# Sliding-window attention with a soft mixture of experts: score groups of 64 queries and eight heads instead of 128 queries and four heads

## The chip, the cores and the metric

The kernel runs on one core of a Trainium2 chip. The metric is device time in microseconds (us) of one execution; lower is better. The engines are called as in the profile: PE is the matrix engine, PEld its loading of the stationary operand (the weights of a matmul), DVE the vector engine, ACT the scalar engine, POOL the GpSimd engine, SP the engine that issues most DMAs.

## What is computed

Batch 8, 8 heads, 576 positions, head size 64. Attention looks back over a window of 128 keys with a bias that grows with the distance, one slope a head; its output, 4608 tokens of 512 values, goes through a soft mixture of 8 experts with 4 slots each.

```python
def _attn_ref(q, k, v):
    B, H, S, D = q.shape
    window = 128
    scale = 1.0 / np.sqrt(D)
    scores = scale * np.matmul(q, k.transpose(0, 1, 3, 2))
    pos = np.arange(S)
    rel = pos[:, None] - pos[None, :]
    slopes = 2.0 ** (-8.0 * (np.arange(H, dtype=np.float32) + 1) / H)
    bias = slopes[:, None, None] * (-np.abs(rel).astype(np.float32))[None, :, :]
    mask = (rel >= 0) & (rel < window)
    scores = np.where(mask, scores + bias[None], -1000000000.0)
    scores = scores - np.max(scores, axis=-1, keepdims=True)
    attn = np.exp(scores)
    attn = attn / (np.sum(attn, axis=-1, keepdims=True) + 1e-09)
    return np.matmul(attn, v).astype(np.float32)

def _moe_ref(x, phi, w1, w2):            # x: tokens, 4608 x 512
    logits = x @ phi                     # 32 slots: 8 experts of 4
    d = softmax of logits over the tokens
    slot_input = d.T @ x
    per expert e: slot_out[e] = relu(slot_input[e] @ w1[e]) @ w2[e]
    c = softmax of logits over the slots
    return c @ slot_out
```

(The last function is written out in short.)

## The kernel before

**Two parts.** The front (up to about 212 us) is attention, with the routing of the experts woven in; the tail loads the last expert weights, runs the experts and combines. Instructions of PE, DVE, ACT, POOL and SP run in the order in which the code emits them (`manual_schedule`), each engine waiting in order for what it needs.

**Groups.** `groups` lists the units of attention: batch b, tile t of 128 positions (t = 4 is the tail of 64), and g. For t < 4, g picks two of the four head pairs, so a group is 128 queries by four heads; t = 4 has one group of 64 queries by eight heads. There are 72 groups: 16 with t = 0, 48 with t = 1 to 3, 8 with t = 4. A head pair sits on the partitions: the even head's 64 dimensions on 0 to 63, the odd one's on 64 to 127 (`half`).

**Scores** (`scores`, L237 to L269) go to a PSUM tile `s4` of four slots (u = 2 x parity + pair) of 256 columns, two banks, double-buffered. For t > 0 the queries are cut into four strips of 32; strip c occupies partitions 32c to 32c+31 and gets the scores of its 160 keys (five blocks of 32) at columns 32c to 32c+159. So the row of query p uses key columns of the previous tile beyond p, and of its own tile up to p. First 8 matmuls of `ramp` with `ones` write the bias (L259), then 16 matmuls of 64 x 32 weights add the scores (L266). An fp32 matmul is two instructions in the profile, each with its weight load. For t = 0 there is no previous tile: 2 bias matmuls (L247) and 4 score matmuls of 64 x 128 weights (L252).

**Softmax.** `merge` on DVE makes one 128-column row of the 256 by a copy under a mask: 128 columns a slot for t = 1 to 3 (L281), 64 for t = 4 (L283); for t = 0 it overwrites the keys above the diagonal with a constant `low` (L279). Then DVE takes the row maximum (L301), scales it (L304), ACT computes the exponentials with their row sums, one slot at a time (`expo`, L357), POOL adds an epsilon (L309), DVE inverts (L313) and multiplies (`normalise`, L317).

**Values.** `flip` turns the four slots on PE (L372), ACT copies them to `pa` (L379), POOL separates the previous tile's part (`pp`, L381) from the own part (`pa`, L383; L386 and L388 for t = 4). `values` (L410) multiplies: for each key tile, pair and parity one matmul, weights 128 keys by 64 dimensions of V, moving 128 queries (64 for t = 4). `x_store` copies a finished tile of x (L426), `x_flip` turns it (L438), `x_keep` copies (L447), and `logits`, `token_*`, `slot_*` do the routing once in four tiles.

**Order.** In iteration i of the main loop DVE gets merge(i), row maximum(i), inverse(i-1), bias(i), normalise(i-1); ACT gets split(i-3) (i-2 in the first iterations), stores and copies of x, then expo(i); PE gets flip(i-3), values(i-4), scores(i+1), then what routing has fallen due. Scores(i+1) needs the PSUM buffer of group i-1, and so its exponentials. The last groups are written out by hand behind the loop; there the weights' loads go into areas that attention has given up (`place`), in an order of their own.

Of the kernel before, what the change touches and what calls it, by code (L numbers as in the profile page):

```python
# [23 lines left out]
NS = E * SPE  # L24
# [11 lines left out]
WIN = P + KB  # L36
NB = S // KB
HW = 512
CW = P + TAIL + NS
WARM = 6  # L40
# [28 lines left out]
def tile_attn_softmoe(  # L69
# [20 lines left out]
    mask_u = cst[:, 0:P].bitcast(I32)  # L90
    mask_t = cst[:, P:P + TAIL].bitcast(I32)
# [14 lines left out]
    ramp = cpool.tile([P, 2, 2, WIN], BF16, name="ramp")  # L106
# [4 lines left out]
    qs = [kq[:, NB * P + 2 * P * i:NB * P + 2 * P * i + 2 * P] for i in range(3)]  # L111
# [61 lines left out]
    def load_q(i, eng=None):  # L173
        b, t, g = groups[i]
        o = 4 * P * t + 2 * P * g
        (eng or nc.sync).dma_start(qs[i % 3], qd[b, :, o:o + 2 * P])
# [29 lines left out]
    with tc.manual_schedule(engines=ORDERED):  # L206
# [6 lines left out]
        nc.gpsimd.memset(cst[:, 0:P], 1.0)  # L213
        nc.gpsimd.affine_select(cst[:, 0:P], cst[:, 0:P], [[1, P]], ALU.is_gt, 0.0, base=0, channel_multiplier=-1)
# [17 lines left out]
        nc.scalar.dma_start(cst[:, P:], cstd)  # L232
# [4 lines left out]
    def scores(i):  # L237
        b, t, g = groups[i]
        s4 = s4s[i % 2]
        parts = [s4[:, 0:2], s4[:, 2:4]]  # L240
        if i == 0:
            parts = [ps_1.tile([P, 2, 2 * P], F32, tag="xp", name="s4_0"), pq[:, 0].rearrange("p (u w) -> p u w", u=2)]
            parts = parts[::-1]
        qt = qs[i % 3].rearrange("p (j w) -> p j w", w=width(t))
        if t == 0:
            for par, rows in enumerate(half):
                nc.tensor.matmul(  # L247
                    parts[par][:, :, 0:P], lhsT=ones[rows], rhs=ramp[rows, g, :, 0:P],
                    start=True, stop=False)
            for jj in range(2):  # L250
                for par, rows in enumerate(half):
                    nc.tensor.matmul(  # L252
                        parts[par][:, jj, 0:P], lhsT=qt[rows, jj], rhs=kall[rows, 0:4, 2 * g + jj],
                        start=False, stop=(jj == 1))
        else:
            strips = [(c // 2, c % 2) if t == 4 else (g, c) for c in range(4)]
            for par, rows in enumerate(half):
                for c, (h, r) in enumerate(strips):
                    nc.tensor.matmul(  # L259
                        s4[32 * c:32 * c + 32, 2 * par:2 * par + 2, 32 * r:32 * r + WIN],  # L260
                        lhsT=ones[rows, 0:32], rhs=ramp[rows, h], start=True, stop=False)
            for jj in range(2):
                for par, rows in enumerate(half):
                    for c, (h, r) in enumerate(strips):
                        m0 = 4 * (t - 1) + r
                        nc.tensor.matmul(  # L266
                            s4[32 * c:32 * c + 32, 2 * par + jj, 32 * r:32 * r + WIN],
                            lhsT=qt[rows, 2 * h + jj if t == 4 else jj, 32 * r:32 * r + 32],
                            rhs=kall[rows, m0:m0 + 5, 2 * h + jj], start=False, stop=(jj == 1))  # L269
        st[groups[i]] = {"s4": s4, "parts": parts}  # L270

    ALL, LO, HI = slice(0, 4), slice(0, 2), slice(2, 4)

    def merge(key, us=ALL):
        t = key[1]
        s4 = st[key]["s4"]
        if t == 0:
            m = len(range(4)[us])
            nc.vector.copy_predicated(merged(key, us), bc(mask_u, 1, m), bc(low, 1, m).to_broadcast([P, m, P]))  # L279
        elif t < 4:  # L280
            nc.vector.copy_predicated(s4[:, :, P:2 * P], bc(mask_u, 1, 4), s4[:, :, 0:P])  # L281
# [841 lines left out]
```

## Time and profile before

| what | value |
|---|---|
| median of 3 runs (lowest, highest) | 289.14 us (288.57, 290.88) |
| the profiled execution | 288.49 us, span of the trace 286.0 us |
| granted TensorE clock, mean | 0.982 |
| busy share of the span: PE, PEld, DVE, ACT, POOL | 89%, 63%, 77%, 72%, 39% |
| bytes moved, mean rate | 72.61 MB, 254 GB/s |

The lines of the profile follow in the prediction. A row of instructions tells line, engine, operation, out<-in with shapes, count, then total busy us, mean ns of one, and the idle time before it with what ended that. A timeline row tells start, duration, engine, line and count, with neighbours of one kind merged. The chain of work that ended last follows the program back from its end, at each step to what released it.

### The profile page before, as it was taken

The page shows a single profiled execution, that of the slowest core. Times are in us where ns is not written, and L with a number is a line of the kernel's source. Part 1 is how long each engine was busy: PE and PEld are TensorE (multiplying, and loading weights), DVE is VectorE, ACT ScalarE, POOL GpSimd, SP SyncE. Part 2 cuts the span into 40 slices and gives each one's busy share as a digit, 9 for nine tenths or more (in the row PEclk, how much of TensorE's full clock was granted, in tenths as well). Part 3 has the DMA queues.
Part 4 walks back from the last instruction along what each step waited for, and adds up shares of the span by engine and source line. Part 5 has one row for each costly group of instructions (what it writes and reads, how often), then busy time and mean ns, then how long its engine had stood idle before and what let it go on. Part 6 is the DMA issues. An engine that isn't in the chain of part 4 may idle for free.

```text
span 286.0 us, 13588 instructions
## 1 busy us (share of the span) xinstructions
PE 253.9 (89%) x5535; PEld 178.9 (63%) x5535; DVE 221.6 (77%) x509; ACT 205.6 (72%) x817; POOL 112.9 (39%) x218
## 2 busy tenths in 40 slices
PE   8588999799979889989979998998979899999990
PEld 4366676676757567667657765766756443687750
DVE  2889989998997999988998998798973352656451
ACT  2888889988888988998898988888783411044460
POOL 2044626662573276257527725466552011000000
PEclk9689999999999999999999999999999999999997
DMA  6645368869885987969797978866574579998997
GB/s 184 218 134 164 100 197 270 276 195 289 285 271 152 305 297 233 278 224 305 218 286 242 328 236 251 278 204 219 165 265 140 169 254 365 411 393 322 362 384 282
DMA packets 36754, 72.61 MB, mean 254 GB/s; under 512 B 4402, under 2 KB 15316, under 8 KB 36692
## 3 DMA queue, kind: packets, MB, share of 16 engines
q1 hardware_dynamic: 35972, 71.24, 75.7%
q8 instruction: 43, 0.70, 1.0%
q10 hardware_dynamic: 720, 0.51, 0.6%
q14 instruction: 19, 0.16, 0.2%
HBM read 62.29 MB, written 9.44 MB: 251 GB/s over the span
## 4 chain that ended last, share of the span: by engine, by line
PE 45%; DVE 23%; ACT 16%; POOL 7%; issue 5%; DMA 2%; DVEq 0%; ACTq 0%; POOLq 0%
ACT area L357 9%; PE xp L410 7%; DVE area L317 6%; DVE s L301 6%; PE s L266 5%; PE op L967 5%; PE hp L930 5%; PE po L992 4%; DVE s L281 3%; POOL area L381 3%; PE pq L372 3%; PE lp L456 2%; DVE s L279 2%; PE s L259 2%; ACT area L379 2%
## 5 line engine op out<-in xcount | busy, mean ns | idle before, releaser
L357 ACT ACTIVATE area<-s,nb 128x128 f32<-128x128 f32 x286 | 102.7, 391 | 13.8 <-DVE nb L304 10.4
L410 PE MATMUL xp<-area 128*64 128x128 f32 (+1 forms) x1104 | 74.5, 272 | 8.4 <-POOL area L381 5.3
L357 ACT ACTIVATION_READ_ACCUMULATOR area<-s,nb 128x1 f32 x286 | 65.4, 229 | 0.0
L410 PEld LDWEIGHTS xp<-area 128*64 128x64 f32 x1104 | 54.1, 137 | 18.0 <-POOL area L381 6.1
L317 DVE TENSOR_TENSOR area<-area,rs 128x512 f32<-128x512 f32 (+1 forms) x73 | 61.0, 836 | 1.6
L301 DVE TENSOR_REDUCE s<-s 128x4 f32<-128x512 f32 x71 | 49.5, 697 | 2.2
L379 ACT COPY area<-pq 128x512 f32<-128x512 f32 (+1 forms) x72 | 43.5, 605 | 10.7 <-PE pq L372 9.0
L266 PE MATMUL s<-kq 64*32 64x160 f32 x1792 | 43.8, 302 | 2.3 <-issue 2.3
L309 POOL TENSOR_SCALAR rs<-sm 128x4 f32<-128x4 f32 x70 | 15.0, 214 | 73.0 <-ACT area L357 71.6
L383 POOL TENSOR_SCALAR_AFFINE_SELECT area<-area 128x512 f32<-128x512 f32 x48 | 41.7, 870 | 3.3
L381 POOL TENSOR_SCALAR_AFFINE_SELECT area<-area 128x512 f32<-128x512 f32 x48 | 35.5, 740 | 15.5 <-ACT area L379 14.6
L281 DVE COPY_PREDICATED s<-cst,s 128x512 f32<-128x512 int32 x48 | 33.1, 689 | 6.1 <-PE s L266 5.6
L372 PE MATMUL pq<-unit_r,area 64*128 64x64 f32 x552 | 31.3, 233 | 3.7 <-ACT area L322 2.8
L266 PEld LDWEIGHTS s<-kq 64*32 64x32 f32 x1792 | 30.1, 107 | 4.1 <-issue 3.5
L372 PEld LDWEIGHTS pq<-unit_r,area 64*128 64x128 f32 x552 | 23.3, 140 | 11.8 <-issue 3.2
L259 PE MATMUL s<-ramp,ones 64*32 64x320 bf16 x448 | 18.7, 311 | 4.8 <-ACT area L357 4.5
L426 ACT COPY area<-xp 128x512 f32<-128x512 f32 (+1 forms) x37 | 21.4, 578 | 0.2
L447 ACT COPY area<-pq 128x512 f32<-128x512 f32 x34 | 20.7, 608 | 0.3 <-PE pq L432 0.3
L438 PEld LDWEIGHTS pq<-unit_r,area 64*128 64x128 f32 x264 | 11.1, 137 | 12.8 <-issue 9.7
L994 ACT COPY ob<-po 128x512 f32<-128x512 f32 x19 | 10.4, 591 | 11.4 <-PE po L992 11.4
L994 DVE COPY ob<-po 128x512 f32<-128x512 f32 x17 | 11.2, 686 | 6.6 <-PE po L992 6.5
L438 PE MATMUL pq<-unit_r,area 64*128 64x64 f32 x264 | 15.2, 233 | 0.9 <-ACT area L379 0.6
(173 smaller groups left out, 329.1 us busy)
## 6 DMA issues: line engine op xcount, KB each, us to landing
w<-w SPq DMA_DIRECT2D x53, 512.0 KB, 5.5
out<-ob SPq DMA_DIRECT2D x36, 256.0 KB, 3.9
kq<-q_t SPq DMA_DIRECT2D x69, 128.0 KB, 3.5
kq<-k_t SPq DMA_DIRECT2D x32, 256.0 KB, 3.9
area<-v_n SPq DMA_DIRECT2D x31, 256.0 KB, 4.2
area<-w SPq DMA_DIRECT2D x8, 512.0 KB, 4.6
area<-v_n SPq DMA_DIRECT2D x12, 128.0 KB, 4.4
kq<-w SPq DMA_DIRECT2D x3, 512.0 KB, 5.9
```

Source lines behind the costliest of these rows:

```text
L259: nc.tensor.matmul(s4[32 * c:32 * c + 32, 2 * par:2 * par + 2, 32 * r:32 * r + WIN], lhsT=ones[rows, 0:32], rhs=ramp[rows, h], start=True, ...
L266: nc.tensor.matmul(s4[32 * c:32 * c + 32, 2 * par + jj, 32 * r:32 * r + WIN], lhsT=qt[rows, 2 * h + jj if t == 4 else jj, 32 * r:32 * r + 32],
L281: nc.vector.copy_predicated(s4[:, :, P:2 * P], bc(mask_u, 1, 4), s4[:, :, 0:P])
L301: nc.vector.tensor_reduce(st[key]["mx"][:, us], merged(key, us), axis=AX.X, op=ALU.max, negate=True)
L317: nc.vector.tensor_tensor(p4, p4, bc(rs, 2, P), op=ALU.mult)
L357: nc.scalar.activation(s["p4"][:, u], merged(key, u), AF.Exp, bias=s["nb"][:, u:u + 1], scale=SCALE, accum_out=s["sm"][:, u:u + 1],)
L372: nc.tensor.transpose(s["pt"][:, u, r], s["p4"][rows, u], ident[rows, rows])
L379: nc.scalar.copy(pa[:, us].rearrange("p u (r w) -> p u r w", r=2), s["pt"][:, us])
L381: nc.gpsimd.affine_select(pp[:, us], pa[:, us], [[0, m], [-1, P]], ALU.is_gt, 0.0, base=0, channel_multiplier=1)
L383: nc.gpsimd.affine_select(pa[:, us], pa[:, us], [[0, m], [1, P]], ALU.is_ge, 0.0, base=0, channel_multiplier=-1)
L410: nc.tensor.matmul(xp[D * par:D * par + D, j, 0:w], lhsT=v_slot[b, t - 1 + ph][:, D * h:D * h + D], rhs=src[:, 2 * par + i] if t < 4 else ...
L438: nc.tensor.transpose(xq[:, j, r], x[rows, j], ident[rows, rows])
```

## The change

A group of t < 4 becomes 64 queries (g picks the half of the tile) by all eight heads. The strips on the partitions are now the four head pairs; a slot (u = 2 x parity + uu) holds one block of 32 queries, uu, with its 160 keys. Slot uu starts at column 224 uu of its bank (OFF), so that the block of keys to be merged lies at the window's end for uu = 0 (block 4 onto block 0) and at its front for uu = 1 (block 7 onto block 11): 32 columns a slot for every t. For t = 0 the blocks of the missing previous tile get no scores but a large negative number, by four matmuls of a row `shut` with `ones`. Keys then lie turned by 64 in half of the slots, which `expo` sets right by reading its 128 columns as two pieces of 64 in reverse order. `flip` writes the slots sorted by uu, POOL's selection works on blocks of 32, and `values` does one matmul for each key tile and head with 64 moving columns. Bias and scores of t = 1 to 4 keep their number and shapes.

```diff
+OFF = 2 * P - KB
+QB = 2 * P
...
-        nc.gpsimd.memset(cst[:, 0:P], 1.0)
-        nc.gpsimd.affine_select(cst[:, 0:P], cst[:, 0:P], [[1, P]], ALU.is_gt, 0.0, base=0, channel_multiplier=-1)
+        nc.gpsimd.memset(shut, 0.0)
+        for par in range(2):
+            nc.gpsimd.memset(shut[64 * par:64 * par + 1, 0:P], LOW)
+        nc.gpsimd.memset(mask, 1.0)
+        for c in range(4):
+            rows = slice(KB * c, KB * c + KB)
+            nc.gpsimd.affine_select(
+                mask[rows, 0], mask[rows, 0], [[-1, KB]], ALU.is_ge, 0.0, base=0, channel_multiplier=1)
+            nc.gpsimd.affine_select(
+                mask[rows, 1], mask[rows, 1], [[1, KB]], ALU.is_gt, 0.0, base=0, channel_multiplier=-1)
...
     def scores(i):
...
+        qt = qs[i % 3].rearrange("p (j u w) -> p j u w", j=NPAIR, u=2)
+        strips = [slice(KB * c, KB * c + KB) for c in range(NPAIR)]
+        for par, rows in enumerate(half):
+            both = parts[par][:, 0:2 * OFF].rearrange("p (u w) -> p u w", u=2)
+            for c, strip in enumerate(strips):
+                nc.tensor.matmul(
+                    both[strip, :, 0:WIN], lhsT=ones[rows, 0:KB], rhs=bc(ramp[rows, c], 1, 2),
+                    start=True, stop=False)
         if t == 0:
             for par, rows in enumerate(half):
+                for uu in range(2):
+                    r = 2 * g + uu
                     nc.tensor.matmul(
+                        parts[par][:, OFF * uu:OFF * uu + WIN], lhsT=ones[rows], rhs=shut[rows, KB * r:KB * r + WIN],
+                        start=False, stop=False)
+        for uu in range(2):
+            r = 2 * g + uu
+            skip = max(4 * (1 - t) - r, 0)
+            m0 = 4 * (t - 1) + r
             for par, rows in enumerate(half):
+                for c, strip in enumerate(strips):
                     nc.tensor.matmul(
+                        parts[par][strip, OFF * uu + KB * skip:OFF * uu + WIN], lhsT=qt[rows, c, uu],
+                        rhs=kall[rows, m0 + skip:m0 + 5, c], start=False, stop=(uu == 1))
...
     def merge(key, us=ALL):
...
+        x = windows(key, us).rearrange("p a (x y) -> p a x y", y=KB)
+        m = x.shape[1]
+        nc.vector.copy_predicated(
+            x[:, :, 0:12:11, :], bc(mask.bitcast(I32), 1, m), x[:, :, 4:8:3, :])
...
     def expo(key, us=ALL):
...
+            src = merged(key, slice(2 * par, 2 * par + 2))[:, par if number[key] else 0, uu]
+            dst = s["p4"][:, u]
+            if uu != key[2]:
+                src = src.rearrange("p (a w) -> p a w", a=2)[:, ::-1]
+                dst = dst.rearrange("p (a w) -> p a w", a=2)
...
     def split(key, us=ALL):
...
+            m, i0 = own.shape[1], 2 * KB * g + KB * (us.start // 2)
             nc.gpsimd.affine_select(
+                prev, own, [[-KB, m], [0, 8], [-1, KB]], ALU.is_gt, 0.0, base=-i0, channel_multiplier=1)
             nc.gpsimd.affine_select(
+                own, own, [[KB, m], [0, 8], [1, KB]], ALU.is_ge, 0.0, base=i0, channel_multiplier=-1)
...
     def values(key, pairs=None, to=None):
...
-        inner = pairs or range(2 if t < 4 else 4)
+        inner = pairs or range(NPAIR)
         for ph in parts:
...
                     nc.tensor.matmul(
+                        xp[D * par:D * par + D, j, TAIL * g:TAIL * g + TAIL],
+                        lhsT=v_slot[b, t - 1 + ph][:, D * h:D * h + D], rhs=(pp, pd)[ph][:, :, par, j],
+                        start=(fresh and (ph, j) == (parts[0], inner[0])),
+                        stop=(done and (ph, j) == (parts[-1], inner[-1])),
                     )
...
     def x_of(b, t):
+        if (b, t) == (last, 0):
+            return halves(5)
...
-        load_weight()
         x_flip(last, 4, pq[:, 1])
         x_flip(last, 0, free[1])
+        load_weight()
         load_weight()
```

The host lays q out by half tiles to match. The tail's hand-written order keeps its steps, but for one load that now stands behind the two `x_flip`, since it fills the area that holds the last x tile now.

PE, a group of t = 0 in the second batch (rows: line, operation, out<-in, moving shape; `xp` is the output of `values`, `kq` holds q and k). Before:

```order
L247 LDWEIGHTS ones
L247 MATMUL s_1_84<-ramp,ones 128x2x128
L252 MATMUL s_1_84<-kq 128x128 x4
L372 MATMUL pq<-unit_r,area 128x64 x8
L410 MATMUL xp<-area 64x128 x8
```

And with the change (eight pairs of rows of L258, the bias, and three pairs of L265 stand ahead of these):

```order
L265 LDWEIGHTS ones
L265 MATMUL s_1_84<-cst,ones 128x160
L274 MATMUL s_1_84<-kq 32x32 x8
L274 MATMUL s_1_84<-kq 32x64 x8
L379 MATMUL pq<-unit_r,area 128x64 x8
L411 MATMUL xp<-area 64x64 x16
```

Two bias matmuls became eight, four of `shut` are new, four score matmuls became 16 narrow ones, and the eight value matmuls of the group in line behind them became 16 of half the width.

DVE, from the group (0, 4) to the first of the next batch. Before:

```order
L283 COPY_PREDICATED s_0_83<-cst,s_0_83 128x4x64
L301 TENSOR_REDUCE s_0_83<-s_0_83 128x4
L313 RECIPROCAL rs<-rs 128x4
L304 TENSOR_SCALAR nb<-s_0_83 128x4
L317 TENSOR_TENSOR area<-area,rs 128x512
L279 COPY_PREDICATED s_1_84<-cst,fine 128x4x128
```

With the change:

```order
L285 COPY_PREDICATED s_0_83<-cst,s_0_83 128x2x2x32
L301 TENSOR_REDUCE s_0_83<-s_0_83 128x2x2
L314 RECIPROCAL rs<-rs 128x4
L305 TENSOR_SCALAR nb<-s_0_83 128x4
L318 TENSOR_TENSOR area<-area,rs 128x512
L285 COPY_PREDICATED s_1_84<-cst,s_1_84 128x2x2x32
```

The order on DVE stands; both copies now move 128 elements a partition, the one of t = 0 without the constant `low` (in `fine`). The rows of t = 1 to 3 change in the same way, from 128x4x128.

More of the change, by code (lines that the diff above doesn't have):

```diff
@@ L89, in tile_attn_softmoe @@
     cst = cpool.tile([P, CW], F32, name="cst")
-    mask_u = cst[:, 0:P].bitcast(I32)
-    mask_t = cst[:, P:P + TAIL].bitcast(I32)
+    mask = cst[:, 0:2 * KB].rearrange("p (u w) -> p u w", u=2)
+    shut = cst[:, 2 * KB:2 * KB + P].bitcast(BF16)
     delta = cst[:, P + TAIL:]
@@ L110, in tile_attn_softmoe @@
     kall = kq[:, 0:NB * P].rearrange("p (n j w) -> p n j w", n=NB, j=NPAIR)
[L111 removed]
+    qs = [kq[:, NB * P + QB * i:NB * P + QB * i + QB] for i in range(3)]
     half = [slice(64 * par, 64 * par + 64) for par in range(2)]
@@ L238, in scores @@
         b, t, g = groups[i]
-        s4 = s4s[i % 2]
-        parts = [s4[:, 0:2], s4[:, 2:4]]
         if i == 0:
-            parts = [ps_1.tile([P, 2, 2 * P], F32, tag="xp", name="s4_0"), pq[:, 0].rearrange("p (u w) -> p u w", u=2)]
-            parts = parts[::-1]
-        qt = qs[i % 3].rearrange("p (j w) -> p j w", w=width(t))
+            parts = [pq[:, 0], ps_1.tile([P, 2 * QB], F32, tag="xp", name="s4_0")]
+        else:
+            parts = [s4s[i % 2][:, 2 * par:2 * par + 2].rearrange("p u w -> p (u w)") for par in range(2)]
@@ L262, in scores @@
[L262 to L269, printed above, removed]
@@ L276, in merge @@
[L276 to L281, printed above, removed]
-        else:
-            nc.vector.copy_predicated(s4[:, :, 0:TAIL], bc(mask_t, 1, 4), s4[:, :, P:P + TAIL])
-    def merged_at(key):
-        return P if 0 < key[1] < 4 else 0
-    def merged(key, us):
-        o = merged_at(key)
-        if number[key] == 0:
-            if isinstance(us, int):
-                return st[key]["parts"][us // 2][:, us % 2, 0:P]
-            return st[key]["parts"][us.start // 2][:, :, 0:P]
-        return st[key]["s4"][:, us, o:o + P]
+        x = windows(key, us).rearrange("p a (x y) -> p a x y", y=KB)
@@ L296, in rowmax, with windows @@
+        m = x.shape[1]
+        nc.vector.copy_predicated(
+            x[:, :, 0:12:11, :], bc(mask.bitcast(I32), 1, m), x[:, :, 4:8:3, :])
+    def windows(key, us):
+        if number[key] == 0:
+            return st[key]["parts"][us.start // 2].unsqueeze(1)
+        return st[key]["s4"]
+    def merged(key, us):
+        x = windows(key, us).rearrange("p a (u w) -> p a u w", u=2)
+        return x[:, :, :, 0:P]
     def rowmax(key, us):
-        if "mx" not in st[key]:
-            o = P - merged_at(key)
-            st[key]["mx"] = st[key]["s4"][:, :, o] if number[key] else work.tile([P, 4], F32, tag="mx", name="mx")
+        if "nb" not in st[key]:
```

97 lines of the change are left out of this document (36 added, 61 removed).

## The prediction

> **What bounds the kernel now.** I read the page first: the engines' shares and the chain of work that ended last.
>
> ```profile
> PE 253.9 (89%) x5535; PEld 178.9 (63%) x5535; DVE 221.6 (77%) x509; ACT 205.6 (72%) x817; POOL 112.9 (39%) x218
> ACT area L357 9%; PE xp L410 7%; DVE area L317 6%; DVE s L301 6%; PE s L266 5%; PE op L967 5%; PE hp L930 5%; PE po L992 4%; DVE s L281 3%; POOL area L381 3%; PE pq L372 3%; PE lp L456 2%; DVE s L279 2%; PE s L259 2%; ACT area L379 2%
> ```
>
> The chain passes from engine to engine; the masked copies that the change shrinks (L281, L279) hold 3% and 2% of it. The busy time by stretches comes next: the front, three pairs of t = 0 groups, and a stretch in which the chain stays on DVE.
>
> ```profile
> core 0: us, PE busy (x) PEld busy (x) DVE busy (x) ACT busy (x) POOL busy (x), PEclk, DMA share, GB/s
> 12.00:212.00 200.00, 183.52 (x4578) 134.94 (x4563) 182.54 (x402) 176.61 (x742) 105.93 (x194) 0.99 0.75 234
> 55.05:60.75 5.70, 3.94 (x98) 3.06 (x98) 5.34 (x13) 4.29 (x20) 4.37 (x7) 1.00 0.72 247
> 81.20:86.90 5.70, 3.94 (x104) 3.06 (x106) 5.35 (x12) 4.41 (x19) 4.36 (x7) 1.00 0.75 239
> 107.67:112.53 4.86, 4.53 (x122) 3.62 (x120) 4.79 (x11) 4.22 (x19) 3.09 (x6) 1.00 0.95 272
> 136.60:150.10 13.50, 12.02 (x339) 8.28 (x337) 13.28 (x32) 12.69 (x58) 5.60 (x13) 1.00 0.84 251
> ```
>
> In the front PE, DVE and ACT are busy 92%, 91% and 88%: three engines near their limit, so that relief of one is soon stopped by the next. Then the waits (us in total, times, the longest), of all engines and of PE alone:
>
> ```profile
> ACT area L357 <- DVE nb L304: 13.8, 24, 3.4
> ```
>
> ```profile
> PE xp L410 <- POOL area L381: 5.3, 6, 1.4
> PE s L259 <- ACT area L357: 4.5, 9, 1.3
> ...
> PE s L266 <- issue: 2.3, 4, 1.0
> PE xp L410 <- POOL area L383: 1.3, 4, 0.4
> ```
>
> PE waits 11.1 us (5.3 + 4.5 + 1.3) for work that comes late out of DVE by way of ACT or POOL; ACT waits 13.8 us for DVE's scaled maximum. These waits are what a faster DVE can give back.
>
> **The change, part by part. The copies.**
>
> ```profile
> L281 DVE COPY_PREDICATED s<-cst,s 128x512 f32<-128x512 int32 x48 | 33.1, 689 | 6.1 <-PE s L266 5.6
> L279 DVE COPY_PREDICATED s<-cst,fine 128x512 f32<-128x512 int32 x15 | 14.9, 997 | 0.1
> L283 DVE COPY_PREDICATED s<-cst,s 128x256 f32<-128x256 int32 x8 | 3.4, 422 | 0.3 <-PE s L266 0.3
> ```
>
> 512 elements cost 689 ns and 256 cost 422, so 267 ns per 256 and 289 ns at 128 elements, if pieces of 32 cost nothing of their own. The first group speaks for that: 256 elements in pieces of 128 took there what L283's pieces of 64 take.
>
> ```profile
> 5.86 0.43 DVE L279 COPY_PREDICATED pq<-cst,fine 128x256 f32<-128x256 int32 x1 [4.18 <-issue]
> ```
>
> The bounds are 155 ns (the line's start) and 422. L279 is dearer than L281 at the same size, and its spread is wide, 425 to 1169 ns with the half ones in it; the new copy reads PSUM under a mask, like L281, which hardly varies, so I price it by L281.
>
> ```profile
> L281 DVE COPY_PREDICATED s<-cst,s x48: 680/688/697, 10.4 to 200.6; 128x512 f32<-128x512 int32 x48
> ```
>
> ```profile
> L279 DVE COPY_PREDICATED s<-cst,fine x16: 425/1122/1169, 6.9 to 209.4; 128x512 f32<-128x512 int32 x15, 128x256 f32<-128x256 int32 x1
> ```
>
> DVE loses 48 x 0.40 = 19.2 us, 16 x 0.71 = 11.3 and 8 x 0.13 = 1.1: 31.6 us of its 182.5. On the chain L281 is 3% of 286 = 8.6 us, of which (689 - 289) / 689 = 58% go: 5.0 us. L279 is 2% = 5.7 us, of which 71% go: 4.1 us. So 9.1 us is the most that this chain gives. How much is kept depends on the neighbours. In the last stretch of the windows four copies are on the chain, the first and the last of them:
>
> ```profile
> 139.66 0.61 DVE s L281
> ...
> 146.95 0.60 DVE s L281
> ```
>
> They would save 4 x 0.4 = 1.6 us, but ACT is busy 12.69 of 13.50 us and leaves 0.8: half is kept. I take half of 5.0, 2.5 us. In the first two t = 0 pairs DVE loses 2 x 0.71 = 1.4 us; ACT needs 4.3 to 4.4 of the 5.70 us and PE, with its added work (below), 3.94 + 0.54 = 4.5: 1.2 us each is kept. In the third pair PE needs 4.53 + 0.54 = 5.07 of 4.86 us: a loss of 0.2. I take two thirds of 4.1, 2.7 us, with PE's added work on t = 0 already inside. Kept: 5.2 us.
>
> **PE, values.** t = 4 already runs the new shape, 32 instructions of 64 columns; behind a group of 16 of 128 columns:
>
> ```profile
> 60.45 1.09 PE L410 MATMUL xp<-area 128*64 128x128 f32 x16
> 61.48 0.33 PE L259 MATMUL s<-ramp,ones 64*32 64x320 bf16 x8
> 61.63 0.73 PE L266 MATMUL s<-kq 64*32 64x160 f32 x32
> ...
> 62.67 1.15 PE L410 MATMUL xp<-area 128*64 128x64 f32 x32
> 63.76 0.33 PE L259 MATMUL s<-ramp,ones 64*32 64x320 bf16 x8
> ```
>
> From start to next start, 1.03 us become 1.09: 6%. On 48 groups 2.9 us of PE, on the chain 6% of L410's 7% (20.0 us) = 1.2 us; I take 1.0. The weight loads go with it:
>
> ```profile
> 60.45 0.85 PEld L410 LDWEIGHTS xp<-area 128*64 128x64 f32 x16
> ...
> 61.51 0.53 PEld L266 LDWEIGHTS s<-kq 64*32 64x32 f32 x32
> ...
> 62.67 1.01 PEld L410 LDWEIGHTS xp<-area 128*64 128x64 f32 x32
> ```
>
> 32 loads take 1.01 us, 32 ns each, though 16 took 53 ns each: at 128 columns they waited for the matmuls. [...]
>
> **PE, scores of t = 0.**
>
> ```profile
> 105.70 0.28 PE L247 MATMUL s<-ramp,ones 64*128 64x256 bf16 x2
> ...
> 105.82 0.61 PE L252 MATMUL s<-kq 64*128 64x128 f32 x8
> ...
> 106.27 0.41 PE L438 MATMUL pq<-unit_r,area 64*128 64x64 f32 x8
> ```
>
> Now 0.57 us from start to start. After: the bias as for other tiles, 0.15 us (61.48 to 61.63); four `shut` matmuls, 640 moving columns in place of L247's 512 in 0.12 us: 0.15; 32 score instructions of 32 to 128 columns, at least the pace of their loads (0.53 us for 32), at most that of 160 columns (0.65). In all 0.83, so +0.27 us (0.25 to 0.4), 0.54 a pair, 4.3 us over 16 groups. It counts in the pairs above.
>
> **Small parts.** PE gets 1440 more matmuls (48 x 16 + 16 x 42) on 5535, each with a load. Their code comes in packets, and the four waits "issue" within the score matmuls (2.3 us) are stalls of PE with nothing else missing:
>
> ```profile
> q8 instruction: 43, 0.70, 1.0%
> ```
>
> 26% more code, 26% more such stalls: 0.6 us (0 to 2.3). [...]
>
> `values` of g = 0 now needs all columns of V. Once, at the last batch, V comes in four half loads and PE waits for it already:
>
> ```profile
> 194.39 2.64 SPq L201 DMA_DIRECT2D area<-v_n  x4
> ...
> 198.97 0.66 PE L410 MATMUL xp<-area 128*64 128x128 f32 x8 [0.90 <-DMA area<-v_n]
> ```
>
> The third and fourth issue come up to 1.3 us (half of 2.64) behind: 0 to 1.3, I take 0.5.
>
> POOL's selections go from pieces of 128 to 32; pieces of 64 cost nothing more so far:
>
> ```profile
> L381 POOL TENSOR_SCALAR_AFFINE_SELECT area<-area 128x512 f32<-128x512 f32 x48 | 35.5, 740 | 15.5 <-ACT area L379 14.6 <-PE xp L410 0.3
> L386 POOL TENSOR_SCALAR_AFFINE_SELECT area<-area 128x512 f32<-128x512 f32 x7 | 5.0, 711 | 3.9 <-ACT area L379 3.1 <-PE xp L410 0.8
> ```
>
> 0 to 10% of L381's 3% of the chain: 0 to 0.9, I take 0.2. Exponentials that read two pieces: ACT's copies of 64-column pieces and of whole rows cost the same, so 0 (up to 0.02 us x 143 = 2.9):
>
> ```profile
> L379 ACT COPY area<-pq 128x512 f32<-128x512 f32 x69 | 42.5, 615 | 9.7 <-PE pq L372 9.0
> ...
> L426 ACT COPY area<-xp 128x512 f32<-128x512 f32 x30 | 18.5, 616 | 0.1
> ```
>
> The mask's and `shut`'s making on POOL lies under the first loads; the moved load waits for two flips of PE in the tail: 0.
>
> **Sum:** -5.2 + 1.0 + 0.6 + 0.5 + 0.2 = -2.9 us. The profiled execution took 288.49 us (span 286.0, 2.5 around it): **285.6 us**, my prediction. The runs' median, 289.14, lies 0.65 above the profiled execution and their lowest, 288.57, at it; against the median it is 1.2% less.
>
> **Rivals.** 1. *The waits go altogether.* PE's 11.1 us of waits for late softmax vanish, and the chain gives its whole 9.1 us less 1.0 for the values: 280.4. For it: PE's whole need in the front is 183.5 + 2.9 + 4.3 = 190.7 of 200 us. Against: ACT's 12.69 of 13.50 us in the DVE stretch.
>
> 2. *PE takes over: slower.* The added 2.9 + 4.3 us of PE, 0.6 of code and 0.5 of V all lie on the path, 8.3 us, since PE is the busiest engine of the front; only half of its 11.1 us of waits goes. 8.3 - 5.6 = +2.7: 291.2. It decides if PE's own waits fall by less than 8.3 us, and shows in t = 0 pairs like the third. Against: in the first two pairs PE has 1.7 us to spare. The loads' pace is its extreme: at 53 ns the 32 loads take 1.70 us, 0.67 more than now, 32 us on 48 groups; PE then needs 183.5 + 32 + 4.3 = 220 us in a front of 200: 308.
>
> 3. *The copy isn't cheap.* Pieces of 32 columns cost as much as 256 elements, 422 ns: DVE saves 267 ns of 689, two thirds of the forecast, and the costs stay: 5.2 x 0.67 = 3.5 - 2.3 = 1.2 us gained, 287.3. For it: no row has such pieces. Against: the equal cost of pieces of 128 and 64.
>
> **How the numbers follow.** Forecast 0.50 (its own range 282.5 to 288), rival 1 0.17, rival 2 0.15 with the slow loads at 0.03 more, rival 3 0.15. The range takes in rivals 1 and 2: 279.5 to 292. About 1% is what a measurement of this kernel tells from no change: 286.2 is that bound. Three quarters of the forecast and rival 1 lie below it: 0.55. The rest of the forecast, rival 3 and a fifth of rival 2 lie within: 0.30. Slower: 0.15.
>
> **What would show it.** Right: copies near 0.29 us, all DVE about 190 us; values at 1.09 us a group of 32; PE's count near 6975; ACT's wait for nb well under 13.8 us; the front's end 3 us earlier and the tail as long as now. Wrong: value blocks over 1.3 us; t = 0 scores over 1 us; PE's wait for POOL and ACT no smaller than 11 us; or an end of the front earlier by 7 us or more.

## The result: slower by 6 and 8%, and the profile after

| | before | changed |
|---|---|---|
| first comparison, 4 runs each: median (lowest to highest) | 289.62 us (288.57 to 290.88) | 309.75 us (304.73 to 313.02) |
| ratio, 95% interval | | 1.0565 [1.0456, 1.0673] |
| second comparison, 8 and 4 runs: median (lowest to highest) | 289.46 us (286.59 to 292.10, and one run of 731.1) | 311.53 us (307.47 to 312.04) |
| ratio, 95% interval | | 1.0763 [1.0669, 1.0856] |
| the profiled execution, span | 288.49 us, 286.0 | 313.02 us, 311.3 |

The ratios leave out runs that lie over 1.5% above the fastest of their kernel: in the first comparison two of the changed kernel (312.19 and 313.02, the profiled one), in the second two of the kernel before (292.10 and 731.1).

The forecast was 285.6 us (279.5 to 292): wrong in size and in sign. The page of the changed kernel, lines that answer to those of before (engines; instruction queue with packets, MB and share; the chain by engine and by line):

```profile
PE 271.8 (87%) x6975; PEld 195.8 (63%) x6975; DVE 194.3 (62%) x509; ACT 208.1 (67%) x817; POOL 120.6 (39%) x228
...
q8 instruction: 55, 0.90, 1.1%
...
PE 68%; ACT 10%; issue 9%; DVE 4%; POOL 3%; DMA 2%; DVEq 0%; ACTq 0%; SPq 0%; POOLq 0%
PE xp L411 17%; PE s L274 11%; PE pq L379 6%; ACT area L364 5%; PE op L971 5%; PE s L258 5%; PE hp L934 5%; PE pq L442 3%; PE po L996 3%; PE ap L518 3%; PE lp L460 2%; ACT area L385 2%; POOL area L390 1%; POOL area L392 1%; DMA area<-v_n 1%
```

DVE lost 27 us of busy time (31.6 were forecast), and the masked copies are nearly off the chain: 0.4% of it, where L281 and L279 had 3% and 2%. But 9% of the chain, 28 us, is now "issue", 14 us more than before: an engine that waits for nothing the profile shows. Which one, PE's waits tell (us in total, times, the longest):

```profile
PE s L274 <- issue: 7.8, 7, 2.8
PE xp L411 <- issue: 5.3, 4, 2.2
PE pq L379 <- issue: 4.1, 3, 2.4
PE s L258 <- ACT area L364: 2.5, 3, 1.2
PE s L258 <- issue: 2.1, 2, 1.2
...
PE xp L411 <- POOL area L390: 1.0, 1, 1.0
```

PE's waits for late softmax, 11.1 us before, are 3.7 us (with 0.2 for POOL's L392). In their place stand 19.3 us of "issue" (7.8 + 5.3 + 4.1 + 2.1), where there were 2.3. They strike scores, values, flips and biases alike, so no operation is the cause. Now DVE and ACT wait for PE:

```profile
DVE s L285 <- PE s L274: 37.9, 35, 3.4
ACT area L385 <- PE pq L379: 32.0, 30, 2.7
```

DVE's copy waited 5.9 us for the scores before (5.6 of them at L281), 37.9 now; ACT's copy 9.0 us for the flips, 32.0 now. One such stall, in order of time (start, us, engine, line; SPq is a DMA being issued):

```profile
66.66 0.42 SPq L141 DMA_DIRECT2D w<-w  x1
...
70.68 0.33 PE L258 MATMUL s<-ramp,ones 64*32 64x320 bf16 x8
70.70 0.49 PEld L274 LDWEIGHTS s<-kq 64*32 64x32 f32 x19
70.81 0.70 PE L274 MATMUL s<-kq 64*32 64x160 f32 x18
74.28 0.78 PE L274 MATMUL s<-kq 64*32 64x160 f32 x14 [2.77 <-issue]
74.29 0.22 PEld L274 LDWEIGHTS s<-kq 64*32 64x32 f32 x13 [3.09 <-issue]
```

A run of 32 score matmuls that needs one strip of keys and one of queries stops after 18 and goes on 2.77 us later. The trace has no semaphore that it waits for, and the first 18 read the same tiles. What is missing, as I read it, is its own instructions. I numbered PE's instructions (matmuls, weight loads and waits on semaphores) from 0 in order of start. The stall that ends at 74.28 is at number 3777. In the front, up to the last row maximum at 234.6 us, there are 18 gaps of over 0.4 us from one start to the next in which PE stands idle and which no wait for another engine or a DMA explains (only for the one that ends at 110.29 the trace names a wait, for DVE, of 0.6 us). All 18 are at 193 plus a multiple of 256: the edges of blocks of 256. So are the four of the kernel before. The instruction queue q8 fits: among 14077 instructions there are 55 such edges, and 55 packets of 16 KB came in; among 11198 there are 43, and 43 packets came in the kernel before. Times of the packets for three of the stalls and, last, an edge without one, from the queue's records and the issues on SP (us; "last weight issue" is the last one ahead of the edge before, and at number 8385 another followed at 162.00):

```
edge          edge before   last weight issue   packet starts   packet ends   PE passes
number 3265    58.11         57.77               60.67           61.55         63.03
number 3777    66.85         66.66               71.88           72.81         74.28
number 8385   160.08        158.97              164.08          165.00        166.41
number 4033    74.28         66.66               75.49           76.42         81.63, no stall
```

In this front each packet behind the first edge started after PE had passed the edge before, 0.39 to 5.03 us later: in these rows 1.21 us later where the last weight load was 7.6 us old, 2.6 to 5.0 us later where 512 KB had been issued within the last 1.1 us. It took 1.0 us in the mean, and at the 18 stalls PE went on 1.22 to 1.65 us after its end, 1.4 in the mean. Of the 637 edges behind a first one in the fronts of all 16 profiles, PE passed 634 no earlier than 1.2 us after the end of their packet (the other three: 0.8, 1.0 and 1.1). So by these numbers, as an estimate, PE stands still if it needs less than that delay and 2.4 us (1.0 + 1.4) for the 256 instructions between two edges.

The clock slowed with the stalls. The windows of the changed kernel (the granted clock is the number behind POOL's count):

```profile
12.00:212.00 200.00, 176.50 (x5213) 133.09 (x5193) 137.26 (x352) 157.91 (x653) 96.02 (x168) 0.94 0.69 211
...
70.00:78.00 8.00, 5.17 (x105) 3.83 (x112) 4.91 (x12) 4.96 (x23) 3.45 (x7) 0.71 0.56 197
```

In the stall from 71.5 to 74.3 the granted clock fell: it was 0.5 for 6.8 us from 73.4 on. In the front of the changed kernel 23.9 us passed at half the clock, 6.8 in the kernel before. The spells are 3.4 or 6.8 us long; those from 12 us on come with gaps on PE of 1.95 to 3.06 us, from start to start, in this profile, and of 1.5 to 3.7 us in the second profile of the changed kernel.

### The profile page after: what moved, and what is told of

It is laid out like the page before. It is cut to its first block, busy times and chain, and to the rows that moved or that the text cites. A ratio compares the mean times of both kernels' runs of the same rounds, so it can differ in the third digit from the quotient of the medians.

```text
span 311.3 us, 16475 instructions
## 1 busy us (share of the span) xinstructions
PE 271.8 (87%) x6975; PEld 195.8 (63%) x6975; DVE 194.3 (62%) x509; ACT 208.1 (67%) x817; POOL 120.6 (39%) x228
## 4 chain that ended last, share of the span: by engine, by line
PE 68%; ACT 10%; issue 9%; DVE 4%; POOL 3%; DMA 2%; DVEq 0%; ACTq 0%; SPq 0%; POOLq 0%
PE xp L411 17%; PE s L274 11%; PE pq L379 6%; ACT area L364 5%; PE op L971 5%; PE s L258 5%; PE hp L934 5%; PE pq L442 3%; PE po L996 3%; PE ap L518 3%; PE lp L460 2%; ACT area L385 2%; POOL area L390 1%; POOL area L392 1%; DMA area<-v_n 1%
## 5 line engine op out<-in xcount | busy, mean ns | idle before, releaser
L411 PE MATMUL xp<-area 128*64 128x64 f32 x1984 | 80.1, 233 | 7.1 <-issue 5.3
L411 PEld LDWEIGHTS xp<-area 128*64 128x64 f32 x1984 | 68.6, 144 | 13.7 <-issue 7.4
L390 POOL TENSOR_SCALAR_AFFINE_SELECT area<-area 128x512 f32<-128x512 f32 (+1 forms) x57 | 47.6, 834 | 41.2 <-ACT area L385 40.1
L274 PE MATMUL s<-kq 64*32 64x160 f32 (+3 forms) x2288 | 56.5, 301 | 7.8 <-issue 7.8
L301 DVE TENSOR_REDUCE s<-s 128x4 f32<-128x512 f32 (+1 forms) x72 | 50.0, 694 | 2.2
L392 POOL TENSOR_SCALAR_AFFINE_SELECT area<-area 128x512 f32<-128x512 f32 (+1 forms) x57 | 49.1, 862 | 3.9
L285 DVE COPY_PREDICATED s<-cst,s 128x128 f32<-128x128 int32 (+1 forms) x72 | 21.0, 291 | 38.2 <-PE s L274 37.9
L379 PE MATMUL pq<-unit_r,area 64*128 64x64 f32 x552 | 33.0, 237 | 6.6 <-issue 4.1
L258 PE MATMUL s<-ramp,ones 64*32 64x320 bf16 x572 | 25.7, 323 | 4.9 <-ACT area L364 2.5
L314 DVE RECIPROCAL rs<-rs 128x4 f32<-128x4 f32 (+1 forms) x73 | 12.6, 172 | 12.1 <-POOL rs L310 12.0
L258 PEld LDWEIGHTS <-ones 64*32 64x32 bf16 x576 | 9.4, 90 | 11.7 <-issue 6.5
```

The source lines that it names most:

```text
L258: nc.tensor.matmul(both[strip, :, 0:WIN], lhsT=ones[rows, 0:KB], rhs=bc(ramp[rows, c], 1, 2), start=True, stop=False)
L274: nc.tensor.matmul(parts[par][strip, OFF * uu + KB * skip:OFF * uu + WIN], lhsT=qt[rows, c, uu], rhs=kall[rows, m0 + skip:m0 + 5, c], star ...
L285: nc.vector.copy_predicated(x[:, :, 0:12:11, :], bc(mask.bitcast(I32), 1, m), x[:, :, 4:8:3, :])
L301: nc.vector.tensor_reduce(st[key]["mx"], merged(key, us), axis=AX.X, op=ALU.max, negate=True)
L379: nc.tensor.transpose(s["pt"][:, 2 * (u % 2) + u // 2, r], s["p4"][rows, u], ident[rows, rows])
L390: nc.gpsimd.affine_select(prev, own, [[-KB, m], [0, 8], [-1, KB]], ALU.is_gt, 0.0, base=-i0, channel_multiplier=1)
```

## The experiments

Theory **F**: code arrives late at the edges of blocks, because the changed PE program passes through a block faster and the packet waits behind the weights' loads. Rival **W**: the change's added matmuls are in themselves too much for PE, and the stalls are only where that shows. The table collects what the traces of all runs gave, one profile each; "stalls" are the number and the sum of gaps of over 0.4 us, from start to start, at block edges in the front (the sum is above that of the waits by "issue", which count idle time alone), "block" is the mean time from edge to edge, "7 batches" the time from the first row maximum to that of group 63, "half" the time at half the clock in the front, "tail" what follows the start of the last row maximum (without loads in the front it waits for them, and is left out). In the diffs "..." stands for lines left out.

```
kernel                        PE matmuls  block   stalls, us   7 batches  half   tail
before                        5535        5.45     4,  3.4     180.0       6.8   76.0
changed                       6975        4.89    18, 24.8     204.0      23.9   76.7
changed, second profile       6975        4.87    16, 23.0     201.6      23.9   76.9
copies alone                  5535        5.46     5,  6.6     180.5      10.2   76.7
values halved                 6431        4.96    14, 16.6     190.1       6.8   75.6
changed, loads early          6975        4.83    13, 21.7     202.7      20.5   77.1
before, loads early           5535        5.62    10, 12.2     187.2       6.8   75.7
one bias                      6479        5.20     9, 13.4     192.1      17.1   78.3
values by tile                6095        5.22     4,  3.2     185.9       3.4   77.9
one bias, values by tile      5599        5.73     0           184.3       3.4   78.7
the same, even                5599        5.63     3,  2.5     179.2       6.8   81.9
changed, half loads           6975        4.71    18, 19.4     195.3       6.8   77.1
changed, no loads in front    6975        4.42     6,  6.4     181.3       3.4   -
before, no loads in front     5535        5.44     0           181.7      13.7   -
before, half loads            5535        5.50     6,  6.1     181.8       6.8   76.2
even, half loads, more areas  5599        5.55     1,  0.9     177.3       0     78.4
```

**The copies alone.** The kernel before, its copies cut to 32 columns; the masking of the other columns is left out.

```diff
...
-            nc.vector.copy_predicated(s4[:, :, P:2 * P], bc(mask_u, 1, 4), s4[:, :, 0:P])
+            nc.vector.copy_predicated(s4[:, :, P:P + KB], bc(mask_u[:, 0:KB], 1, 4), s4[:, :, 0:KB])
...
```

> The kernel before, with its masked copies cut to 32 columns a slot; the rest of the masking is left out. PE's code is as before. Theory F (PE reaches the edge of a block of 256 instructions before the next block's code has come in): 283 us (280 to 286), the gain of the shorter copies at the old number of PE instructions; PE's waits by issue in the front stay near 2.3 us, no stall over 1.3 us. Rival W (the change made PE's own matmul work larger than priced): the same, 283, since that work isn't in here. If the copies were off the path all along: 289, and then neither theory has a gain to explain away.

Measured: 285.35 us, ratio 0.9897 [0.9834, 0.996]. The copies are worth 3.5 us (288.87 - 285.35), with 5.2 us of "issue" waits still in the profile. They are a gain by themselves, of 1%. The 15 copies of t = 0 (L279, still of the constant in `fine`) take 642 ns each here; in the change they take 292, so its copies may be worth more than 3.5 us.

**Values halved.** The kernel before, each value matmul of 128 columns as two of 64: the change's shape without its layout.

```diff
...
+                    for o in range(0, w, TAIL):
+                        nc.tensor.matmul(
+                            xp[D * par:D * par + D, j, o:o + TAIL], lhsT=v_slot[b, t - 1 + ph][:, D * h:D * h + D],
+                            rhs=src[:, 2 * par + i, o:o + TAIL] ...
...
```

> The kernel before, with each value matmul of 128 columns done as two of 64: 896 more matmuls and as many loads, nothing else. F: packets of code 43 to 50, PE's waits by issue 2.3 to 8 to 14 us, all at the same place in a block of 256 instructions; 298 us (294 to 303). W: PE's busy time rises by 10 us or more without such waits, value blocks of 32 take well over 1.1 us: about 300. By the prediction's price (0.06 us a group): 292.

Measured: 300.69 us, ratio 1.0389 [1.0307, 1.047]. 896 more matmuls in the old kernel bring 12 us and the stalls with them, each again at 193 plus a multiple of 256:

```profile
PE s L266 <- issue: 3.7, 3, 2.3
PE xp L411 <- issue: 3.5, 5, 0.9
...
PE pq L372 <- issue: 1.2, 2, 1.0
...
PE s L252 <- issue: 1.0, 1, 1.0
```

They reach the scores (L266, L252) and flips, which this edit did not touch. The moving columns are the same as before; what grew is the number of instructions. The time alone does not tell the theories apart (298 and 300 were expected), but the waits do: "issue" has 9.7 us of PE, 7.4 more than before. The rest is PE's own work: a block of 32 values takes 1.13 us in the median, where 16 of double width took 1.03, about 5 us on 48 groups, and not "well over 1.1" as W had it.

**The loads early.** The weights' loads go out from group 4 to 42 instead of 10 to 66, first in the changed kernel, later in the kernel before.

```diff
-WEND = 66
-W0 = 10
+WEND = 42
+W0 = 4
```

> The changed kernel, with the 36 early weight loads of 512 KB put into iterations 4 to 41 instead of 10 to 66; the later half of the front has none. F, with the code's packet waiting behind those loads in the DMA engines: PE's waits by issue gather in the stretch with the loads (15 us or more between 13 and 140 us) and are under 3 us in all between 145 us and the end of the loop; 300 to 310 us in all. F without that (the code comes too late whatever else is loaded): the waits in both halves alike. W: no difference between the halves beyond the clock.

Measured: 307.09 us (304.74 to 309.67), ratio 1.061 [1.0528, 1.0692]. The stalls moved with the loads: 13 of them, up to 3.4 us, all before 149 us and none in the last three batches of the front. The control:

> The kernel before with the expert weights' loads issued early, as in e3 (first at group 4, last at 42): the control to e3. F: 289 to 291 us, a few more stalls than before in the first half and none in the last batches; there (batches 5 to 7) its time against e3's 25.7, 27.7 and 22.5 us tells what the change is worth where no code is late: 0 to 2 us a batch in the change's favour. W: the changed kernel is the slower there too, by 1 us a batch or more.

Measured: 293.3 us (291.14 to 295.27), ratio 1.016 [1.0081, 1.0239], a little above what F said: with loads this dense the kernel before has stalls too, ten of them, 12.2 us, all but one of 0.7 us while the loads run. The last three batches, where no load is left, took 25.5, 26.7 and 22.9 us, in the changed kernel 25.7, 27.7 and 22.5: 75.1 against 75.9. Where hardly any code is late the change is worth nothing that two profiles could tell (0.3 us a batch against it): the lower end of F's gain of 0 to 2 us a batch, and not W's loss of 1 or more.

**One bias.** The changed kernel with the biases of a bank and `shut` in one matmul, 496 matmuls fewer.

```diff
...
-            for c, strip in enumerate(strips):
-                nc.tensor.matmul(
-                    both[strip, :, 0:WIN], lhsT=ones[rows, 0:KB], rhs=bc(ramp[rows, c], 1, 2),
-                    start=True, stop=False)
...
+            tilted = bc(tilt[rows, 0:WIN], 1, 2) if t else tilt[rows, o:o + 2 * WIN].rearrange("p (u w) -> p u w", u=2)
+            nc.tensor.matmul(both[:, :, 0:WIN], lhsT=pairs[rows], rhs=tilted, start=True, stop=False)
...
```

> The changed kernel, with the bias of the four strips and the large negative number of t = 0 in one matmul a bank (five rows of a table, weights that pick a row for each strip): 496 matmuls and as many loads fewer in the loop, the same sums. F: packets of code 55 to 51, PE's waits by issue 19.6 to 10 to 13 us, 297 us (292 to 301). W: only the four matmuls of the negative number go, 0.15 us in 16 groups: 303 to 304.

Measured: 307.91 us (306.78 to 309.06), ratio 1.0652 [1.0576, 1.0729]: the time expected was missed. The stalls fell as expected, and seven batches took 192.1 us instead of 204.0. The eighth gave half of it back: 30.8 us instead of 24.3, with 6.8 us at half the clock and these rows in it:

```profile
206.35 0.57 PE L398 MATMUL xp<-area 128*64 128x64 f32 x12 [2.05 <-issue]
213.74 0.45 PE L398 MATMUL xp<-area 128*64 128x64 f32 x8 [1.05 <-DMA area<-v_n]
215.92 0.69 PE L398 MATMUL xp<-area 128*64 128x64 f32 x8 [1.73 <-DMA area<-v_n]
```

V's half loads came 2.8 us late there, the wait that the prediction had priced at 0.5. The profile accounts for one execution; that the other runs lose time at the same place is not shown.

**Values by tile, and both.** The changed kernel again as the base; then the values of both halves of a tile in one matmul of 128 columns (three buffers for `pa` and `pp`, one weight area less); then this together with one bias.

```diff
...
+        whole = t < 4 and to is None
+        if whole and g == 0:
+            return
...
-                        xp[D * par:D * par + D, j, TAIL * g:TAIL * g + TAIL],
-                        lhsT=v_slot[b, t - 1 + ph][:, D * h:D * h + D], rhs=(pp, pd)[ph][:, :, par, j],
+                        xp[D * par:D * par + D, j, cols],
+                        lhsT=v_slot[b, t - 1 + ph][:, D * h:D * h + D], rhs=(pp, pd)[ph][:, :, :, par, j] if whole else (pp, pd)[ph][:, :, par, j],
...
```

> The changed kernel unaltered, as the base of the next three on the same chip. 307 us (304 to 313); PE's waits that end in "issue" 14 to 20 us in all, against 2.3 in the kernel before; the instruction queue at 53 to 56 packets.

Measured: 311.53 us, 55 packets, 17.3 us of "issue" on PE.

> The changed kernel with the values of both halves of a tile in one matmul of 128 columns again (about 880 instructions of PE fewer, with as many loads; nothing else of the change undone). Theory F (code arrives too late at the edges of its blocks): 292 us (288 to 298), waits by "issue" 8 us at most. Rival W (the change's matmuls are themselves too much work for PE, the waits only show where): the values were priced at +2.9 us of PE, so no lower than 304.

Measured: 299.23 us (295.1 to 301.55), ratio 1.0266 [1.0167, 1.0365]. The waits by "issue" are 2.3 us, as F said, and 12 us are back, but F expected 19. A new wait of PE, for the exponentials, stands against them:

```profile
PE s L259 <- ACT area L365: 20.1, 26, 1.3
```

> The changed kernel with the values of a tile in one matmul and one bias matmul a bank; PE has then about as many instructions as in the kernel before (5600 against 5535), while the small masked copies stay. F: the stalls go and the copies' gain is left, 284.5 us (281 to 288), waits by "issue" about 3 us. W: 302 us, since neither the scores of t = 0 nor the work on the other engines gets less.

Measured: 295.7 us (294.43 to 299.27), ratio 1.0286 [1.019, 1.0382]. No stall is left, and still neither theory's time came. The same wait is there in PE's waits of this last kernel:

```profile
PE s L255 <- ACT area L352: 18.6, 26, 1.2
PE pq L367 <- ACT area L311: 2.1, 1, 2.1
```

The edit itself seemed to have made it: PE did no values behind a tile's first group and 1.97 us of them behind its second, so in turn it ran ahead of the exponentials and held them up.

**The same, even.** Head pairs 0 and 1 behind the tile's second group, pairs 2 and 3 behind the next one; four buffers, one more weight area gone.

```diff
...
+        if whole and pairs is None and postponed(b, t):
+            pairs = range(0, 2)
...
```

> The kernel of e6 with the values of a tile (t = 0 to 2) split by head pairs over two groups: pairs 0 and 1 behind the tile's second group, pairs 2 and 3 behind the next one, so that PE has about the same work in each group; four buffers for pa and pp, one weight area less. In e6 no wait by "issue" was left, but PE waited 18.6 us in 26 pieces for the exponentials. If that was the uneven share of the values (U): those waits fall to 5 us or less, the batches to 25 us, and the time to 287 us (283 to 290), the tail 2 us longer than the kernel before's. If the change's own work on PE is what is too much (W), the batches stay near 26.6 us and the time at 295.

Measured: 295.14 us (293.88 to 296.13), ratio 1.0182 [1.0138, 1.0226]. The time is the one that W named, but the waits and the front are not W's: with the share evened the wait for the exponentials is 2.7 us.

```profile
PE xp L415 <- POOL area L378: 3.1, 5, 0.8
PE s L255 <- ACT area L352: 2.7, 8, 0.9
...
PE s L262 <- issue: 1.4, 2, 1.0
```

Seven batches took 179.2 us, 25.6 each, where W had 26.6; the kernel before's took 180.0. What is left is the tail, 81.9 us against 76.0: two areas for weights have become buffers, and their loads come later. I had allowed 2 us for it.

**Half loads.** Each weight load of the front as two of 256 KB, at two places of the group; in the changed kernel and later in the kernel before.

```diff
...
-        nc.sync.dma_start(wt[units[n]], (w1d, w2d)[m][e, :, UW * k:UW * (k + 1)])
...
+        if half:
+            nc.sync.dma_start(dst[:, 0:cut], src[:, 0:cut])
+            open_half.append(lambda: nc.sync.dma_start(dst[:, cut:], src[:, cut:]))
...
```

> The changed kernel with each 512 KB weight load of the front issued as two of 256 KB at two places of the group: same bytes, same instructions of PE. If a packet of code waits behind the bytes of the load last issued (F), its waits halve: "issue" 5 to 10 us in all, none over 1.5 us, little of the half clock, 297 us (293 to 302). If the bytes a second are what delays the packets (B), nothing changes: 307 to 313 us.

Measured: 305.02 us (302.95 to 306.72), ratio 1.0517 [1.0446, 1.0588], between the two. There are as many stalls, 18, but the longest is 2.2 us, not 3.1, and half the clock lasted 6.8 us, not 23.9. In the changed kernel 9 of 46 packets started over 3 us after their edge, here 1; over 2 us it was 19 in both. So here the long delays came with the large loads, but loads of half the size still left those of 2 us.

> The kernel before with each weight load of the front issued as two of 256 KB. In the changed kernel this gave 2% only, as it made stalls shorter but not fewer. F: the kernel before has 2.3 us of such stalls; they go to about 1 us, and 288 us (286.5 to 290) comes out, no more than 1% better. B (what counts is the bytes, or more descriptors of half the size cost time): 290 us or more.

Measured: 288.75 us (286.84 to 291.78), ratio 1.0018 [0.998, 1.0056]: nothing. The stalls did not go to 1 us as F said: 6 with 6.1 us in this profile. They cost nothing that the time shows; that the kernel before's 11 us of other waits on PE take them up would explain it, and is not shown.

**No loads in the front.** All the loads of groups 10 to 65 go out at group 68. The whole is longer by the tail's wait for them; the front is what counts.

```diff
-        if i >= W0 and loaded[0] < NW and (NW - loaded[0]) * (WEND - W0 - 2) >= NW * (WEND - i):
-            load_weight()
         if groups[i] == (last, 3, 1):
             load_v(True)
+            for _ in range(NW):
+                load_weight()
```

> The changed kernel with none of the expert weights' loads in the front: all that were spread over groups 10 to 65 are issued at group 68, so that the tail waits for them and the whole is longer; what counts is the front, from the first row maximum to that of group 63 (eighth batch's first), and PE's waits by "issue" in it. F (the stalls are packets of code behind those loads): no stall over 0.5 us but for a few, 3 us in all at most, and the front within 3 us of the next run's. W (the change's own work on PE): still 10 us or more behind the next run's.

> The kernel before with the same loads moved to group 68: the control. Its seven batches took 180.1 us with the loads; F: 2 to 5 us less, since its own few stalls and their half clock go. W: 180 us.

Measured: 331.52 us (330.47 to 332.56) for the changed kernel, 331.2 (331.16 to 331.25) for the one before: the same. Seven batches took 181.3 and 181.7 us. The windows of the changed kernel, then of the one before (up to the new loads):

```profile
12.00:190.00 178.00, 170.18 (x5238) 128.81 (x5222) 139.16 (x355) 157.37 (x658) 96.93 (x168) 1.00 0.47 138
```

```profile
12.00:190.00 178.00, 165.11 (x4082) 120.68 (x4067) 161.36 (x354) 155.46 (x657) 90.94 (x168) 0.96 0.46 138
```

In 178 us the changed kernel issued 5238 matmuls and was busy for 170; with the loads it had been 5213 in 200 us. All of its matmuls are there, nothing of the change is undone, and the loss is gone: W falls. Two things were not as F expected. Six stalls of 6.4 us in all are left in the changed kernel, where 3 us at most was said, since packets still start 1.39 us after their edge in the mean there. And the kernel before got no faster (181.7 against 180.0), though its stalls went; two half-clock spells of 3.4 us, after gaps of 1.6 and 1.4 us on PE, took their place.

**Both made good.** The even kernel with half loads, and with two of the freed buffers taken for weights in the tail.

```diff
...
         values(gc, to=quarters(free[0]))
+        load_weight()
...
```

> The kernel of e8 with half loads, and with two more of the freed areas used in the tail for weights. e8's front was as long as the kernel before's (204.2 against 203.8 us), its tail 5.9 us longer because two weight areas had gone to buffers. Tail as supposed: 78 to 79 us, and with the last stalls gone from the front 289 us (286 to 292). If the tail's length is not a matter of these areas: 294 us.

Measured: 288.55 us (287.27 to 292.28), ratio 0.9973 [0.9938, 1.0008]. One stall is left, the front is 2 to 3 us shorter than the kernel before's and the tail 2.4 us longer. Nothing that was tried is faster than the kernel before by more than the measurement tells, apart from the copies alone, which leave masking out.

## Why the prediction was wrong

The step that failed is the term "26% more code, 26% more such stalls: 0.6 us (0 to 2.3)". It took the number of stalls to grow with the number of packets. But a stall is what a delay leaves over a bound, and the bound moved. A block of 256 instructions took 5.45 us in the kernel before; less the 2.4 us of a packet's way, a delay of up to 3.0 us was hidden. In the changed kernel without loads, where few edges stall, a block takes 4.42 us in the mean, and 2.0 us are hidden. The delays themselves hardly changed, 1.86 and 1.98 us in the mean: before, 4 of 35 were over 3 us, and there were 4 stalls; after, 19 of 46 were over 2 us, and there were 18. That the counts come so near is partly chance, since a block's time varies: three of the four stalls before had delays of 2.3 to 2.4 us, behind blocks for which PE needed only 3.7 to 4.5 us, and of the 18 after 14 had over 2 us. So 17 us more of waits came (19.3 less 2.3) where 0.6 was priced, and the half clock behind them came on top: 17 us more of it at 0.5, by my estimate up to half of that lost. 17 + 8.5 is about the 24 us by which the first seven batches were longer; PE's added work and what it waits less for other engines about cancel, as the runs without loads show. In the kernel before without loads no stall came at 36 edges.

The rest, point by point:

- **Copies**: right. Priced 289 ns each; the groups by shape of the changed kernel:

```profile
L285 DVE COPY_PREDICATED s<-cst,s 128x128 f32<-128x128 int32 x71 | 20.8, 292 | 38.2 <-PE s L274 37.9
```

- **What they release**: ACT's wait for the scaled maximum fell from 13.8 to 4.0 us and PE's for softmax from 11.1 to 3.7: two thirds of the way on which rival 1 had them go. The stalls hide a part of ACT's: in the runs without loads it fell from 14.3 to 9.2 us, PE's from 12.0 to 4.6. Of the 5.2 us to be kept, the copies alone gave 3.5, with those of t = 0 still at 642 ns.

- **Values**: right. **Scores of t = 0**: too low. In the timeline of the changed kernel without loads:

```profile
105.59 0.33 PE L258 MATMUL s<-ramp,ones 64*32 64x320 bf16 x8
105.85 0.32 PE L265 MATMUL s<-cst,ones 64*128 64x160 bf16 x4
106.10 0.41 PE L274 MATMUL s<-kq 64*32 64x32 f32 x32
106.44 0.47 PE L442 MATMUL pq<-unit_r,area 64*128 64x64 f32 x8
```

  and in that of the changed kernel itself, for a tile's second half:

```profile
87.11 1.15 PE L411 MATMUL xp<-area 128*64 128x64 f32 x32
88.19 0.33 PE L258 MATMUL s<-ramp,ones 64*32 64x320 bf16 x8
88.46 0.32 PE L265 MATMUL s<-cst,ones 64*128 64x160 bf16 x4
88.70 0.61 PE L274 MATMUL s<-kq 64*32 64x96 f32 x32
89.25 0.46 PE L379 MATMUL pq<-unit_r,area 64*128 64x64 f32 x7
```

  From start to next start the values take 1.08 us (priced 1.09). A first half of t = 0 takes 0.85 us (105.59 to 106.44), a second one, with more columns, 1.06 (88.19 to 89.25), over the 1 us that I had named as wrong; priced 0.83. That is 0.12 us a group, 2 us in all, and near the upper end of the 0.25 to 0.4 us that had been added.

- **POOL's selections**: priced at 0 to 10% more, the first of the two takes 849 ns for its 55 whole groups where 740 stood, 15%; the second 874 where 870 stood. **V's half loads**: 0.3 us of one weight load's wait in the profile after, 2.8 us of PE's with one bias. **Tail**: 76.7 us, as long as before but for 0.7.

- **The sum without the code**: -2.9 - 0.6 = -3.5 us. The kernels without loads say 0 (331.52 against 331.2, 181.3 against 181.7). With 6.4 us of stalls in the one front and 6.8 us more of half clock in the other it can't be settled to the us. The last batches with the loads early say the same (75.9 against 75.1): most of the 3.5 us that the copies give did not come. That PE's added work took it back is argued, not shown.

- **Rivals**: 2 had the sign right, slower, by the wrong price: it said 291.2 us from PE's own work, which less the copies' gain comes to about nothing in the runs without loads. Its condition, that PE's waits for other engines fall by less than 8.3 us, was met by a little (7.4), but two thirds of them went and not half, and the loss came from elsewhere. The 53 ns a load of its extreme are those of a row of 16 loads; in the changed kernel the 32 loads of a group took 1.01 us, 32 ns each (PEld, L411, at 87.11 us).

## What to carry to other kernels

In these traces an instruction of PE cost more than its time on the engine: it had to come in, 256 to a packet of 16 KB (43 packets for 11198 instructions, 55 for 14077), and the next packet started only about the edge of the block before (at most 0.5 us ahead of it, 5.0 us behind it at number 3777). Where PE runs at a pace near that (here 256 instructions in 4.4 us, against delay, transfer and start of 3.3 us in the mean in the kernel before without the loads and 4.4 us in the changed kernel with them), work out the hidden margin and compare it with the delays in the trace, instead of scaling the stalls that are there; a margin smaller by a third went with 18 stalls in place of 4. Halving a matmul's moving columns for the sake of another engine is to be priced so, above all where bulk loads run beside it (18 stalls of 24.8 us in the changed kernel with them, 6 of 6.4 us without), and with the clock in view: 20 of 26 gaps of over 1.8 us on PE came with half the clock here (below).

## What the runs showed that I had not expected

- PE's code stalls sat at fixed places: behind the first 193 instructions of the trace and behind each 256 more, in all 14 profiles that have any, whatever instruction stands there.
- A packet of 16 KB took 1.0 to 1.1 us in the mean. In the kernel before it started 0.93 us after the edge in the mean with no weights' loads about (35 packets) and 1.86 with them, in the changed kernel 1.39 and 1.98 (46 packets), and 5.0 us behind a load of 512 KB (number 3777); at the stalls PE went on 1.4 us after its end. What delays the packets that are late without the weights' loads is open. In a few cases (18 of 637, in other profiles than the two of the first comparison) a packet started up to 0.5 us ahead of the edge as counted here.
- In the fronts of all profiles, from 12 us on, 20 of 26 gaps of over 1.8 us on PE (from start to start) came with 3.4 or 6.8 us at half the clock, and 3 of 28 gaps of 1.4 to 1.8 us. One of those without was of 2.4 us, from 122.9 on, in the kernel before with early loads.
- Stalls don't add up in the time: 12.2 us of them cost the kernel before 4 us, 6.1 us nothing, while 25 us, with the half clock, went with the whole 24 us by which the front of the changed kernel grew.
